# Attention scores on four array quarters and two PSUM banks, with a new order of products, new ordering rules and a table of due times

## The chip, the cores and the metric

One core of a Trainium2 chip runs the whole program. The metric is device time in microseconds (us): 1652.56, the median of three runs (1651.66 to 1653.05).

## The reference

```python
# q, k, v: 8 batches x 8 heads x 576 tokens x 64, float32
scores = scale * (q_chunk @ k_chunk.T)        # chunks of 64 tokens, 9 per head
attn = exp(scores - max); attn = attn / (sum(attn) + 1e-9)
x = (attn @ v_chunk), as 4608 tokens x 512
h = maximum(x @ moe_w_in, 0)                  # 512 x 2048
y = (h * h) @ moe_w_out                       # 2048 x 512
gate = 1 / (1 + exp(-(y @ moe2_w_gate)))      # 512 x 1536
out = (gate * (y @ moe2_w_val)) @ moe2_w_out  # 1536 x 512, result 4608 x 512
```

## The kernel before

Everything is first written down as jobs (`Plan.job`): an engine, an estimated cost, the buffers read and written, and for TensorE (PE) work a nominal time. `Plan.run` plays these jobs through on its own estimates, once, while the kernel is built, and so fixes one order per engine and the SBUF and PSUM places of all buffers; `Plan.emit` then issues them in that order. PE work comes in two streams: "main", the big products, taken in the order written, and "att", the attention jobs, each with a nominal time counted in main-stream work. At every free moment of PE the ready candidate with the smallest due time goes. The other engines take the ready job with the smallest due time; a job that must place a new buffer waits until it is near its due time (`LOOK`, `NEAR`). All DMAs are issued from SP's queue (L415), in that one order.

**Attention** (`attention`): 36 tiles of 128 tokens, two chunks of 64 each. For q and k of the first tiles, four PE transposes (L768) turn the data; later tiles are loaded in a shape that VectorE (DVE) turns (L751; such a load, `ql` or `kl`, is 16 DMAs). Then come the scores (L785, 16 products of 64x64x64, each two matmul records, so 32 records a tile, into one PSUM bank), on DVE the maximum (L803) and the subtraction (L804), Exp on ScalarE (ACT, L806), sum and normalisation on DVE (L807 to L812), a transpose on PE (L819), a copy (L422), the product with v (L835, "mix", also 32 records, but on all four quarters of the array and in two banks), and two copies into `raw` (L850). `raw` holds the tokens of a pair of blocks: 6 tiles, 768 tokens. The scores use, for either chunk c and head half r, the array rows of half r and the output partitions of half r: two diagonal quarters.

**The main stream.** The first pair of blocks runs as plain products (`plain_unit`) against the weights `wia` and `wil`, while the weights are still being turned from 64-bit words into float32 and split in two fp32r parts. The other pairs run as Strassen-like units of seven products P1 to P7 (`Unit`, L641; six matmuls of 384 columns each in the first stage, 512 or 256 columns in the gate and value stage). Bank U of a unit collects P1, P6, P7 and P4 one on the other; after P6 ACT copies it to `c`, after P7 DVE adds it to `b` (L451), so P7 must wait for the copy and P4 for the addition. `units` interleaves a unit with the last one: P1, P7 of the last, P2, P5, P3 and P4 of the last, P6. The two w_out stages (`Long`, L961) do the same seven products, each over all k parts, in the order P1, P4 of the last, P2, P5, P6, P3, P7; P7 and P4 need a difference of inputs from POOL (or DVE), P3 and P2 need none. Stages in time: start-up to 35 us, plain products to about 123, first units to 501, `Long` to 850, gate and value units to 1380, `Long` to the end.

## Time and profile before

| | |
|---|---|
| time, median of 3 runs | 1652.56 us |
| span of the profiled execution | 1649.1 us |
| PE busy | 1614.4 us, 98% |
| DVE busy | 1363.8 us, 83% |
| ACT, POOL busy | 983.6 us, 817.1 us |
| granted TensorE clock, mean | 0.994 |

The profile is of one execution, whose span runs from the first to the last instruction. Matmuls are pipelined and their ends are modelled, so what a piece of PE work costs is read from the distance between starts, not from the busy time. What ended a wait is inferred from semaphore events.

### The profile page before, as it was taken

How to read it: one execution, taken by the hardware profiler on the slowest of the kernel's cores; microseconds unless marked ns; L12 is line 12 of the kernel's file. 1: busy time of each engine (PE TensorE's matmuls, PEld its weight loads, DVE VectorE, ACT ScalarE, POOL GpSimd, SP SyncE). 2: the span in 40 equal slices, each digit the busy share in tenths (PEclk: the TensorE clock that was granted, in tenths of full speed). 3: DMA queues.
4: the chain of work that ended last, by engine and by line, in shares of the span. 5: the costliest groups of instructions: out<-in, count | busy, mean ns of one | idle time of the engine just before them, and what ended most of it. 6: DMA issues, size and time to landing. Idle time of an engine off the chain costs nothing.

```text
span 1649.1 us, 30839 instructions
## 1 busy us (share of the span) xinstructions
PE 1614.4 (98%) x10500; PEld 1459.8 (89%) x10500; DVE 1363.8 (83%) x2002; ACT 983.6 (60%) x1968; POOL 817.1 (50%) x636
## 2 busy tenths in 40 slices
PE   7999999999999999999999999999999999999998
PEld 6998998999999999999988888888888888788887
DVE  6988885777769999999999897754787737999995
ACT  6876765666666565566666565544564545455543
POOL 1253412030334444544469786643676637767672
PEclk9999999999999999999999999999999999999999
DMA  9955666577674765675865846496456687665562
GB/s 226 274 153 143 164 194 170 159 207 193 215 261 156 220 200 176 222 235 194 315 218 205 287 152 208 157 356 226 152 174 217 204 318 246 178 197 128 165 174 47
DMA packets 390798, 333.36 MB, mean 202 GB/s; under 512 B 234736, under 2 KB 325616, under 8 KB 390640
## 3 DMA queue, kind: packets, MB, share of 16 engines
q1 hardware_dynamic: 390640, 331.38, 65.1%
q8 instruction: 83, 1.36, 0.4%
q14 instruction: 75, 0.61, 0.1%
HBM read 209.13 MB, written 122.16 MB: 201 GB/s over the span
## 4 chain that ended last, share of the span: by engine, by line
PE 87%; DVE 6%; SPq 2%; issue 2%; DMA 1%; ACT 1%; POOL 1%; DVEq 0%; ACTq 0%
PE bank L641 47%; PE bank L961 35%; SPq L415 2%; PE bank L785 2%; PE bank L835 1%; PE bank L819 1%; PE bank L768 1%; DMA wraw__378<-in_moe_w_in_dram 0%; DVE T__2002 L442 0%; DMA gd<-b__2597 0%; DMA gd<-b__4693 0%; DMA g__6282<-gd 0%; DVE T__1999 L442 0%; DVE T__10402 L442 0%; DVE x__14497 L442 0%
## 5 line engine op out<-in xcount | busy, mean ns | idle before, releaser
L507 POOL TENSOR_TENSOR wf__1799<-wf__1799,wr__1407 128x512 int32<-128x512 int32 x16 | 21.2, 1325 | 181.6 <-DVE wf__1799 L500 85.1
L507 POOL TENSOR_TENSOR wf__7363<-wf__7363,wr__6457 128x512 int32<-128x512 int32 x18 | 26.1, 1450 | 79.1 <-ACT x__8870 L437 19.4
L507 POOL TENSOR_TENSOR wf__6801<-wf__6801,wr__6457 128x512 int32<-128x512 int32 x18 | 27.2, 1509 | 66.3 <-DVE wf__6801 L500 45.3
L451 POOL TENSOR_TENSOR raw__514<-raw__674,raw__514 128x384 f32<-128x384 f32 x20 | 23.6, 1202 | 42.4 <-DVE B__741 L442 26.7
L488 ACT ACTIVATE wr__6457<-wr__6457 128x512 int32<-128x512 uint32 x36 | 23.9, 664 | 0.0
L442 DVE TENSOR_TENSOR wx__7300<-ws__7420,wx__7300 128x512 fp32r<-128x512 f32 x18 | 19.0, 1053 | 0.0
L491 DVE TENSOR_SCALAR wf__7363<-wf__7363 128x512 f32<-128x512 f32 x18 | 10.4, 576 | 10.0 <-ACT wf__7363 L484 10.0
L442 DVE TENSOR_TENSOR wx__7585<-ws__7420,wx__7585 128x512 fp32r<-128x512 f32 x18 | 18.3, 1017 | 0.0
L451 POOL TENSOR_TENSOR ws__7420<-wf__6801,wf__7363 128x256 f32<-128x256 f32 x18 | 16.7, 928 | 2.3 <-DVE wx__7585 L442 1.1
L500 DVE SCALAR_TENSOR_TENSOR wf__7363<-wr__6457,wf__7363 128x512 int32<-128x512 int32 x18 | 16.2, 901 | 0.1
L491 DVE TENSOR_SCALAR wf__6801<-wf__6801 128x512 f32<-128x512 f32 x18 | 10.6, 588 | 6.8 <-ACT wf__6801 L484 6.8
L507 POOL TENSOR_TENSOR w__647<-w__647,wraw__374 128x512 int32<-128x512 int32 x1 | 1.3, 1294 | 29.9 <-DVE w__647 L500 29.9
L451 POOL TENSOR_TENSOR ws__7420<-ws__7420,wf__6801 128x256 f32<-128x256 f32 x18 | 15.4, 857 | 1.3
L442 DVE TENSOR_TENSOR wx__7423<-wf__7363,wx__7423 128x256 fp32r<-128x256 f32 x18 | 14.4, 801 | 1.8 <-ACT wx__7423 L437 1.8
L493 DVE TENSOR_SCALAR wf__7363<-wf__7363 128x512 int32<-128x512 int32 x18 | 14.5, 807 | 0.6
L484 ACT ACTIVATE wf__6801<-wr__6457 128x512 f32<-128x512 f32 x18 | 12.0, 666 | 5.0 <-POOL ws__7420 L451 2.3
L484 ACT ACTIVATE wf__1799<-wr__1407 128x512 f32<-128x512 f32 x16 | 10.6, 663 | 4.3 <-DMA wf<-wf__1799 4.2
L500 DVE SCALAR_TENSOR_TENSOR wf__6801<-wr__6457,wf__6801 128x512 int32<-128x512 int32 x18 | 12.8, 713 | 0.1
L850 ACT ACTIVATE raw__514<-bank 128x256 f32<-128x256 f32 x36 | 12.0, 384 | 1.0 <-PE bank L835 0.5
L484 ACT ACTIVATE wf__7363<-wr__6457 128x512 f32<-128x512 f32 x18 | 11.8, 656 | 1.1 <-DVE wx__7423 L442 0.9
L451 POOL TENSOR_TENSOR raw__514<-raw__514 128x384 f32<-128x384 f32 x10 | 12.4, 1260 | 0.0
L850 ACT ACTIVATE raw__674<-bank 128x256 f32<-128x256 f32 x36 | 11.9, 380 | 0.2
(5702 smaller groups left out, 6477.2 us busy)
## 6 DMA issues: line engine op xcount, KB each, us to landing
ad<-wx__7300 SPq DMA_DIRECT2D x27, 512.0 KB, 4.6
ad<-wx__7585 SPq DMA_DIRECT2D x27, 512.0 KB, 4.1
wr__1407<-in_moe_w_out_dram SPq DMA_DIRECT2D x16, 512.0 KB, 4.4
wr__6457<-in_moe_w_gate_dram SPq DMA_DIRECT2D x12, 512.0 KB, 5.4
wr__6457<-in_moe_w_val_dram SPq DMA_DIRECT2D x12, 512.0 KB, 5.6
wr__6457<-in_moe_w_out_dram SPq DMA_DIRECT2D x12, 512.0 KB, 4.1
ad<-wx__7423 SPq DMA_DIRECT2D x18, 256.0 KB, 4.4
wf<-wf__1799 SPq DMA_DIRECT2D x16, 256.0 KB, 4.6
```

What stands on the lines that cost most here:

```text
L415: nc.sync.dma_start(out=a, in_=b)
L442: lambda: nc.vector.tensor_tensor(out=lo(), in0=at(src, n, F32, off), in1=hi().bitcast(F32), op=ALU.subtract),
L451: eng, cost(eng, n), lambda: e.tensor_tensor(out=o(), in0=a(), in1=b(), op=op),
L484: nc.scalar.activation(out=at(w), in_=t[:, :, 1].bitcast(F32), func=ACTF.Abs)
L488: nc.scalar.activation(out=low, in_=low.bitcast(U32), func=ACTF.Copy, scale=2.0**-29)
L491: nc.vector.tensor_scalar_max(at(w), at(w), TINY)
L500: nc.vector.scalar_tensor_tensor(out=wi, in0=words()[:, :, 1], scalar=-0x40000000, in1=wi, op0=ALU.bitwise_and, op1=ALU.bitwise_or,)
L507: nc.gpsimd.tensor_tensor(out=wi, in0=wi, in1=words()[:, :, 0], op=ALU.add)
L641: nc.tensor.matmul(out=o, lhsT=at(op, P, F32R, wi * size + half * HB + kk * P), rhs=at(xb, n, F32R, xi * xsize + off), start=(first and kk ...
L785: nc.tensor.matmul(out=o[part, 2 * hp + c, :], lhsT=qv[part, hp, tok], rhs=kv[part, hp, tok], start=True, stop=True,)
L850: nc.scalar.activation(out=o[:, :, a:a + CH], in_=i, func=ACTF.Copy)
L961: nc.tensor.matmul(out=at(ps[m], n), lhsT=at(w, P, F32R, wi * size + half * HB + m * P), rhs=at(x, n, F32R, xi * n), start=(first and kp = ...
```

## The change

It has seven parts. (1) The scores of chunk c go to a bank of their own, and the second chunk's products cross over: array rows of half r, output partitions of half 1 - r; the four products of one head pair stand next to each other. Maximum and subtraction become two operations each, on 256 columns; the mix reads its weights from the crossed places. (2) The planner adds a cost when PE goes from full-array to quarter products and back (`ENTER`, `LEAVE`), and while in quarter products prefers another such job that is up to 6 us early (`STAY`). (3) A load or store on SP that is not due within 10 us is held while the estimated DMA backlog is over 2 us (`CALM`, `DEEP`). (4) The nominal times of the attention jobs come from a table, and a mix waits as a job for the readers of `raw` and for the mix before. (5) `units` takes P2 ahead of P7 of the last unit, and the last unit and the end of a stage have an order of their own; so has the last unit of `long_units`. (6) The plain products read their second weight from the place of `t`, whose real contents, with `s` and `d`, are made after the plain unit; the buffer `wil` goes. (7) The token operands of the first stage are placed ahead of everything.

```diff
@@ -135,7 +135,7 @@
         events, order = [], []
         t, dma, shift, done = 0.0, 0.0, 0.0, 0
         port = {"DVE": 0.0, "POOL": 0.0, "debt": 0.0}
-        stall, why = 0.0, {}
+        small = False
 
         def place(b):
 
@@ -194,7 +194,7 @@
             return False
 
         def begin(j):
-            nonlocal dma, done, shift
+            nonlocal dma, done, shift, small
             j.start, j.started = t, True
             done += 1
             order.append(j)
@@ -206,7 +206,10 @@
 
 
                 cost = j.cost
-                if j.shared and j.eng == "DVE":
+                if j.eng == "PE":
+                    cost += self.ENTER * (j.shared and not small) + self.LEAVE * (small and not j.shared)
+                    small = j.shared
+                elif j.shared and j.eng == "DVE":
                     cost += port["debt"] + min(0.82 * cost, 0.45 * max(0.0, port["POOL"] - t))
                     port["debt"], port["DVE"] = 0.0, t + cost
                 elif j.shared:
@@ -231,7 +234,7 @@
                         cands = [jobs[n] for _, n in ready["PE"]]
                         if heads["main"] < len(streams["main"]):
                             cands.append(jobs[streams["main"][heads["main"]]])
-                        for j in sorted(cands, key=lambda j: j.due):
+                        for j in sorted(cands, key=lambda j: (j.due - self.STAY * (small and j.shared), j.n)):
                             if not j.left and take(j):
                                 if j.stream == "main":
                                     heads["main"] += 1
@@ -253,8 +256,8 @@
                         j = jobs[n]
                         tries += 1
                         need = sum(b.size for b in j.allocs if b.at is None)
-                        ok = True
-                        if need:
+                        ok = not (e == "SP" and due - t + shift > self.CALM and dma - t > self.DEEP)
+                        if need and ok:
                             if due - t + shift > (j.look or (self.LOOK if e == "SP" else self.NEAR)):
                                 ok = False
                             else:
@@ -305,7 +308,9 @@
         self.order = order
         return order
 
-    LOOK, NEAR, HOLD, FAR, FLOOR = 90.0, 20.0, 8.0, 55.0, 8 * 1024
+    LOOK, NEAR, HOLD, FAR, FLOOR = 90, 20, 8, 55, 8192
+    ENTER, LEAVE, STAY = 0.1, 0.15, 6
+    CALM, DEEP = 10.0, 2.0
 
     def stuck(self, t, free, ready, heads, streams, shift):
         live = {}
@@ -574,25 +579,28 @@
             return lambda: at(buf, HB, F32, i * HB)
 
         finished("a")
+
+        def rest(look):
+            s1, s2, s3, s4 = ((sums, i) for i in range(4))
+            for o, x, y, op in (
+                (s1, a21, a22, ALU.add),
+                (s2, s1, a11, ALU.subtract),
+                (s3, a11, a21, ALU.subtract),
+                (s4, a12, s2, ALU.subtract),
+            ):
+                binary("POOL", part(*o), part(*x), part(*y), op, HB, [sums],
+                       {x[0], y[0]} | ({sums} if o[1] else set()), look=look)
+            split(ops["s"], sums, BLK, look=look)
+            finished("s")
+            split(ops["t"], sums, BLK, off=BLK, look=look)
+            finished("t")
+            split(ops["d"], b, HB, off=HB, look=look)
+            finished("d")
+
         if late:
-            ops["l"] = Buf(8 * BLK, name="wil", op=True)
-            split(ops["l"], b, BLK, look=look)
-            look = late
-        s1, s2, s3, s4 = ((sums, i) for i in range(4))
-        for o, x, y, op in (
-            (s1, a21, a22, ALU.add),
-            (s2, s1, a11, ALU.subtract),
-            (s3, a11, a21, ALU.subtract),
-            (s4, a12, s2, ALU.subtract),
-        ):
-            binary("POOL", part(*o), part(*x), part(*y), op, HB, [sums],
-                   {x[0], y[0]} | ({sums} if o[1] else set()), look=look)
-        split(ops["s"], sums, BLK, look=look)
-        finished("s")
-        split(ops["t"], sums, BLK, off=BLK, look=look)
-        finished("t")
-        split(ops["d"], b, HB, off=HB, look=look)
-        finished("d")
+            split(ops["t"], b, BLK, look=look)
+            return ops, lambda: rest(late)
+        rest(look)
         return ops
 
     def weight_rows(src, f, name, keep=True, look=None, raws=None):
@@ -753,6 +761,46 @@
             job("DVE", 0.1 + 0.15 * n, go, [r], [o])
             i += n
 
+    TIMES = [
+        (-40, -40, -38, -34, -32),
+        (-38, -38, -36, -32, -30),
+        (-36, -36, -34, -30, -28),
+        (-34, -34, -32, -28, -26),
+        (-32, -32, -30, -26, -24),
+        (-30, -30, -28, -24, -22),
+        (19.5, 15, 17.5, 21.5, 23),
+        (-0.75, 9, 0.25, 3.25, 26.5),
+        (20.25, 15.25, 20.5, 13, 27.5),
+        (24.25, 25.25, 30.5, 27, 30),
+        (13.75, 19.75, 13.5, 24.5, 28.5),
+        (19.75, 30.5, 36.25, 38.25, 52),
+        (69.25, None, 51.5, 67.5, 72.25),
+        (70.25, None, 64.75, 65.5, 72.5),
+        (82.5, None, 83.5, 88.75, 92.75),
+        (88.485, None, 89.526, 94.731, 98.895),
+        (96.75, None, 94.75, 100.25, 105.75),
+        (96.5, None, 96.5, 102.75, 105),
+        (126.25, None, 131.75, 132.25, 134.5),
+        (136, None, 139.75, 149.75, 150),
+        (131.75, None, 142, 145.75, 144.5),
+        (149, None, 156.75, 160.5, 161.75),
+        (155.25, None, 156, 157.25, 169),
+        (160.75, None, 157, 166.75, 172.5),
+        (186.5, None, 188.75, 187.75, 192.5),
+        (191, None, 200, 203.5, 208.5),
+        (184.75, None, 189, 200.75, 206.25),
+        (203.5, None, 204.5, 209.75, 216.25),
+        (217.75, None, 211.75, 212.25, 225.75),
+        (224.75, None, 222.5, 232, 229),
+        (253.25, None, 250.25, 254.75, 264.25),
+        (242.5, None, 240.25, 255.25, 259),
+        (251.25, None, 255.75, 264.75, 276),
+        (272.75, None, 265.25, 278, 288.75),
+        (255, None, 261, 278.25, 285.25),
+        (276.25, None, 275.5, 291, 289),
+    ]
+    before_mix = []
+
     def attention(t, raw, col, nominal):
         turned = {}
         for src, nm in ((k, "k"), (q, "q")):
@@ -769,28 +817,31 @@
                         out=at(ps, P, F32, hp * P), in_=at(r, P, F32, hp * P), identity=ident
                     )
 
-            job("PE", 0.45, go, [r], [ps], stream="att", at=nominal("k"))
+            job("PE", 0.45, go, [r], [ps], stream="att", at=nominal(nm))
             copy(lambda o=o: at(o), [o], lambda ps=ps: at(ps, BLK), [ps], BLK)
         qT, kT = turned["q"], turned["k"]
-        ps = psum("ps_s")
+        ps_s = [psum(f"ps_s{c}") for c in range(2)]
+
+        def chunk(c):
+            return at(ps_s[c], HB).rearrange("p (h k) -> p h k", h=HP)
 
         def scores():
             qv, kv = (at(x).rearrange("p (h t) -> p h t", h=HP) for x in (qT, kT))
-            o = at(ps, BLK).rearrange("p (h c) -> p h c", h=H)
-            for c in range(2):
-                tok = slice(CH * c, CH * c + CH)
-                for hp in range(HP):
+            o = [chunk(c) for c in range(2)]
+            for hp in range(HP):
+                for c in range(2):
+                    tok = slice(CH * c, CH * c + CH)
                     for r in range(2):
-                        part = slice(CH * r, CH * r + CH)
+                        part, to = (slice(CH * x, CH * x + CH) for x in (r, r ^ c))
                         nc.tensor.matmul(
-                            out=o[part, 2 * hp + c, :],
+                            out=o[c][to, hp, :],
                             lhsT=qv[part, hp, tok],
                             rhs=kv[part, hp, tok],
                             start=True,
                             stop=True,
                         )
 
-        job("PE", 1.0, scores, [qT, kT], [ps], stream="att", at=nominal("S"))
+        job("PE", 0.53, scores, [qT, kT], ps_s, stream="att", at=nominal("S"), shared=True)
         mx = sbuf(128, "mx")
         a = sbuf(BLK, "a")
 
@@ -800,9 +851,19 @@
         def col8(b, i):
             return at(b, H, F32, i * H).rearrange("p (h o) -> p h o", o=1)
 
-        job("DVE", 0.7, lambda: nc.vector.tensor_reduce(out=col8(mx, 0), in_=heads(ps), axis=AX.X, op=ALU.max), [ps], [mx])
-        job("DVE", 0.7, lambda: nc.vector.tensor_tensor(
-            out=heads(a), in0=heads(ps), in1=col8(mx, 0).to_broadcast([P, H, CH]), op=ALU.subtract), [ps, mx], [a])
+
+        def largest(c):
+            return at(mx, HP, F32, c * HP).rearrange("p (h o) -> p h o", o=1)
+
+        def of_chunk(c):
+            return at(a, BLK).rearrange("p (h c k) -> p h c k", h=HP, c=2)[:, :, c, :]
+
+        for c in range(2):
+            job("DVE", 0.45, lambda c=c: nc.vector.tensor_reduce(
+                out=largest(c), in_=chunk(c), axis=AX.X, op=ALU.max), [ps_s[c]], [mx])
+            job("DVE", 0.35, lambda c=c: nc.vector.tensor_tensor(
+                out=of_chunk(c), in0=chunk(c), in1=largest(c).to_broadcast([P, HP, CH]), op=ALU.subtract),
+                [ps_s[c], mx], [a])
         job("ACT", 0.63, lambda: nc.scalar.activation(out=at(a), in_=at(a), func=ACTF.Exp, scale=scale), [a], [a])
         job("DVE", 0.7, lambda: nc.vector.tensor_reduce(out=col8(mx, 1), in_=heads(a), axis=AX.X, op=ALU.add), [a], [mx])
 
@@ -835,12 +896,15 @@
                         nc.tensor.matmul(
                             out=o[c][CH * r:CH * r + CH, hp, :],
                             lhsT=vv[part, 2 * hp + r, :],
-                            rhs=av[part, hp, r, :],
+                            rhs=av[part, hp, r ^ c, :],
                             start=True,
                             stop=True,
                         )
 
-        job("PE", 0.8, mix, [aT, vr], ps_x, stream="att", at=nominal("X"))
+        mixed = job("PE", 0.66, mix, [aT, vr], ps_x, stream="att", at=nominal("X"), shared=True)
+        mixed.deps.update(raw.readers)
+        mixed.deps.update(before_mix)
+        before_mix[:] = [mixed.n]
         off = (t % TILES) * P
 
         def put(c):
@@ -903,7 +967,7 @@
         for row, col in ((0, 0), (1, 0), (0, 1), (1, 1)):
             ps = psum("C")
             for half in range(2):
-                multiply(ps, ops["al"[row]], half, xs[f"B{half + 1}{col + 1}"], n, half == 0, per)
+                multiply(ps, ops["at"[row]], half, xs[f"B{half + 1}{col + 1}"], n, half == 0, per)
             finish(u, row, col, ps)
 
 
@@ -911,7 +975,13 @@
         last = None
         for make in [*todo, None]:
             u, more = make() if make is not None else (None, None)
-            for who, p in ((u, "P1"), (last, "P7"), (u, "P2"), (u, "P5"), (last, "P3"), (last, "P4"), (u, "P6")):
+            if u is None:
+                steps = [(last, p) for p in ("P2", "P7", "P3", "P4")]
+            elif make is todo[-1]:
+                steps = [(u, "P1"), (u, "P5"), (last, "P7"), (last, "P3"), (u, "P6"), (last, "P4")]
+            else:
+                steps = [(u, "P1"), (u, "P2"), (last, "P7"), (u, "P5"), (last, "P3"), (last, "P4"), (u, "P6")]
+            for who, p in steps:
                 if who is not None:
                     who.stage(p)
                 if p == "P4" and more is not None:
@@ -1014,7 +1084,10 @@
         last = None
         for make in [*todo, None]:
             u = make() if make is not None else None
-            for who, p in ((u, "P1"), (last, "P4"), (u, "P2"), (u, "P5"), (u, "P6"), (u, "P3"), (u, "P7")):
+            steps = [(u, "P1"), (last, "P4"), (u, "P2"), (u, "P5"), (u, "P6"), (u, "P3"), (u, "P7")]
+            if make is todo[-1]:
+                steps = [(u, "P1"), (last, "P4"), *((u, p) for p in ("P5", "P6", "P2", "P7", "P3"))]
+            for who, p in steps:
                 if who is not None:
                     who.stage(p)
             last = u
@@ -1066,18 +1139,11 @@
         SLOT = 6 * per1
         raw1 = [sbuf(KD * BL1, f"raw{c}", top=True) for c in range(2)]
         slots1 = {name: [Buf(8 * BL1, top=True, name=name, op=True) for _ in range(2)] for name in B_OF.values()}
-        WHEN = {"k": 0, "S": 1, "T": 6, "X": 10}
-
+        plan.first.extend(b for some in (slots1.values() if isinstance(slots1, dict) else slots1) for b in some)
         def attend(s):
-            for i in range(2 * TILES):
-                def nominal(what, i=i):
-                    slot = 7 * i + WHEN[what]
-                    if s == 0:
-                        return -40.0 + 2.0 * i + {"k": 0, "S": 2, "T": 6, "X": 8}[what]
-                    if s == 1:
-                        return slot * SLOT * 8 / 7
-                    return span0 + (s - 2) * span + slot * SLOT
-                attention(2 * TILES * s + i, raw1[i // TILES], i // TILES, nominal)
+            for t in range(2 * TILES * s, 2 * TILES * (s + 1)):
+                i = t % (2 * TILES)
+                attention(t, raw1[i // TILES], i // TILES, dict(zip("kqSTX", TIMES[t])).get)
 
         def blocks1(raws):
             return {(r, c): [(raws[c], (2 * r + kk) * BL1) for kk in range(2)] for r in range(2) for c in range(2)}
@@ -1104,10 +1170,11 @@
             for op, (src, off) in zip(first_xs[name], x):
                 split(op, src, BL1, off=off)
         for g in range(G1):
-            w1[g] = weight_group(w1i, g, G1, f"wi{g}", True, look=30.0, late=30.0)
+            w1[g], rest = weight_group(w1i, g, G1, f"wi{g}", True, look=30.0, late=30.0)
             if g == 1:
                 attend(1)
             plain_unit(w1[g], first_xs, BL1, per1, finish0(g))
+            rest()
         state = {}
 
         def unit1(s, g):
```

## Rows read from the trace of the kernel before

**Rows 1.** Page: busy us, share, instructions.
```profile
PE 1614.4 (98%) x10500; PEld 1459.8 (89%) x10500; DVE 1363.8 (83%) x2002; ACT 983.6 (60%) x1968; POOL 817.1 (50%) x636
```

**Rows 2.** Windows: stretch, length, busy us by engine, clock, DMA share, GB/s.
```profile
34.70:131.00 96.30, 94.97 (x930) 89.05 (x928) 88.43 (x146) 77.65 (x160) 42.52 (x38) 1.00 0.78 208
131.00:440.00 309.00, 302.17 (x2976) 284.44 (x2977) 233.14 (x442) 199.09 (x434) 68.47 (x62) 0.99 0.66 183
...
70.00:80.00 10.00, 10.00 (x115) 9.37 (x114) 9.84 (x15) 8.36 (x18) 4.38 (x4) 1.00 1.06 317
```

**Rows 3.** Timeline of PE around scores: start, length, what, records.
```profile
208.37 0.69 PE L641 MATMUL bank<-T__2050,wid__2730 128*128 128x384 f32 x3
208.99 1.15 PE L785 MATMUL bank<-kT__1941,qT__2812 64*64 64x64 f32 x32
210.06 0.79 PE L641 MATMUL bank<-T__1999,wis__1503 128*128 128x384 f32 x3
210.70 0.68 PE L641 MATMUL bank<-T__2002,wis__1503 128*128 128x384 f32 x3
211.22 0.68 PE L641 MATMUL bank<-B__741,wia__861 128*128 128x384 f32 x3
```

**Rows 4.** Timeline of PE around a mix.
```profile
218.53 0.69 PE L641 MATMUL bank<-T__2002,wis__1597 128*128 128x384 f32 x3
219.14 0.69 PE L835 MATMUL bank<-aT__643,v__2931 64*64 64x64 f32 x32
219.76 0.79 PE L641 MATMUL bank<-B__741,wia__1015 128*128 128x384 f32 x3
220.40 0.68 PE L641 MATMUL bank<-B__744,wia__1015 128*128 128x384 f32 x3
```

**Rows 5.** Windows of the scores' line L785: PE, PEld, clock, DMA, GB/s.
```profile
34.70:440.00 405.30, 35.27 (x960) 31.10 (x960) 0.99 0.69 189
```

**Rows 6.** Waits of PE: us in total, times, longest.
```profile
PE bank L785 <- ACT kT__2177 L422: 3.9, 1, 3.9
PE bank L961 <- ACT x__8116 L437: 3.5, 1, 3.5
...
PE bank L641 <- DVE T__2002 L442: 1.6, 3, 0.8
PE bank L641 <- DVE b__11090 L451: 1.4, 1, 1.4
...
PE bank L641 <- ACT c__2138 L422: 0.8, 1, 0.8
...
PE bank L641 <- ACT c__10973 L422: 0.2, 1, 0.2
```

**Rows 7.** Timeline of all engines, 277 to 290 us.
```profile
277.90 5.43 SPq L415 DMA_DIRECT2D ql__3745<-in_q_dram  x11
...
287.50 0.49 ACT L422 ACTIVATE b__2597<-bank 128x384 f32<-128x384 f32 x1 [6.90 <-DMA gd<-b__2597]
...
289.35 1.98 PE L785 MATMUL bank<-kT__2177,qT__3890 64*64 64x64 f32 x32 [3.86 <-ACT kT__2177 L422]
```

**Rows 8.** Timeline, 845 to 847 us: DVE and PE.
```profile
845.59 0.54 DVE L451 TENSOR_TENSOR b__8437<-b__8437,bank 128x384 f32<-128x384 f32 x1
846.23 1.28 PE L961 MATMUL bank<-x__6308,wod__6323 128*128 128x384 f32 x6 [3.50 <-ACT x__8116 L437]
```

**Rows 9.** Timeline, 979 to 985 us: PE and DVE, units of 256 columns.
```profile
979.91 0.98 PE L641 MATMUL bank<-T__10970,v__9698 128*128 128x256 f32 x6
...
983.97 0.41 DVE L451 TENSOR_TENSOR b__11090<-b__11090,bank 128x256 f32<-128x256 f32 x1
...
984.43 0.38 PE L641 MATMUL bank<-T__10993,v__9685 128*128 128x256 f32 x1 [1.38 <-DVE b__11090 L451]
```

**Rows 10.** Windows of the maximum's line L803: DVE busy us.
```profile
0.00:1649.00 1649.00, 24.81 (x36) 0.99 0.66 202
```

**Rows 11.** Chain of work that ended last, 0 to 40 us: start, length, what.
```profile
24.45 6.11 DMA wraw__378<-in_moe_w_in_dram
```

## Prediction

> **What bounds the kernel now.** I read the busy table first: PE is busy 98% of the span, DVE 83%, ACT 60%, POOL 50% [rows 1]. An engine at 98% with the full clock (1.00 in the stretches of rows 2) leaves two ways to a shorter time: less PE work, or fewer PE waits. The table of PE waits comes next [rows 6]: after start-up no cause is above 4 us, and the idle times of PE from 36 to 1637 us, added up, are some 17 us. So the question for each part is how many microseconds of PE's own queue it takes away, and whether what feeds PE can follow. The windows answer the second: DVE is busy 88.4 of 96.3 us in the stretch of the plain products and 233 of 309 us in the units behind it [rows 2]. The first 35 us are no PE stage: their chain runs through SP's queue into the loads of q, k, v and the first weights, the last a load of 6.1 us [rows 11].
>
> **What the scores cost PE.** Undisturbed main groups of three matmuls start 0.52 us apart (210.70, 211.22) [rows 3]. From the start of the last main group ahead of the scores (208.37) to the second group behind them (210.70) are 2.33 us, of which two groups are 1.04; the scores cost 1.29 us. By the same count the mix costs 220.40 - 218.53 - 1.04 = 0.83 us [rows 4], with the same 32 records of 64 columns. Inside, the scores' records start (1.15 - 0.22)/31 = 0.030 us apart, taking 0.22 us as the modelled end of the last, the mix's (0.69 - 0.22)/31 = 0.015: two at a time against four. So 0.96 us of the scores is 32 records at their pace and 0.33 us entering and leaving; of the mix 0.48 and 0.35. The new order gives the scores the mix's pattern, four quarters and two banks. They should cost 0.83 us, 0.46 less. 960 records, 30 tiles, lie among main work [rows 5]: **30 x 0.46 = 13.8 us less**. The other six lie in start-up, where the loads set the end; I count them at nothing (between -2 and +2 us).
>
> Here a rule of the Trainium skill speaks against the change. "TensorEngine Tiling (Array Packing)", PSUM Pressure, says that different row tiles can't access the same PSUM bank simultaneously; the new order sends both row halves into each bank. By it the pairs of a bank would go one after the other and nothing of the 13.8 us would come. The old scores do just that already, both row halves into one bank, and their records start as densely as two at a time [rows 3]; the trace doesn't bear the rule out, for outputs on different partitions.
>
> **Scores and mixes side by side.** The visits stand alone today, each paying its 0.33 to 0.35 us of entering and leaving [rows 3, 4]. With `STAY` a second quarter job that is ready and up to 6 us early follows at once. From the table's due times of tiles 6 to 35, 60 jobs, I counted groups: 33 if all are ready, 45 if data take 3 us more to be ready. So 15 to 27 visits fall away. No row shows two of them side by side; the saving for each lies between nothing and 0.35 us. I take 18 at 0.30, nearer the upper end, because the cost sits at the change between the two kinds and not inside: **-5.4 us** (0 to -9.5). The same page, Key Properties, says that changing the tiling mode drains the engine; by it the whole 0.35 is saved and the sum is 0.9 us lower.
>
> **The order of the products.** P7 waits for ACT's copy of U after P6 (the `c` waits). Between P6 and P7 stands one product, P1; with P2 moved ahead there are two. Six `c` waits, 0.8 down to 0.2 us, sum 3.1 (the first and the last stand in [rows 6]); one more product (1.04 us or more; 0.79 in narrow units, below) covers each, also at the end of the stages, where P4 and P2 come between. **-3.1 us**. The price: P4 waits for DVE's addition after P7 (the `b` waits), and its cover falls from three products to two. There are four such waits, sum 2.5, the longest 1.4 us [rows 6]. In that one P7 starts at 979.91, DVE gets to the addition at 983.97, and P4 starts at 984.43 after 1.38 us of idling [rows 9]; a product there takes (4.52 - 1.38)/4 = 0.79 us. If DVE comes no earlier, each of the three in narrow units grows by 0.79, and a few in wide ones begin: up to +4. The planner's due time for the addition moves ahead with P4, so I take **+1.9** (0 to +4).
>
> **The last `Long` unit.** P4 follows P7 directly, so it waits for both additions: DVE begins the first at 845.59, and P4 starts at 846.23 after 3.50 us idle [rows 8]. The new order puts P3 between, which needs no difference from POOL and lasts over 8 us. **-3.5 us**, and what is next there, P4's differences from POOL, gains the time of P3 too. At the kernel's end the same swap changes who is second last, not the last chain: nothing.
>
> **SP's queue.** The longest PE wait, 3.9 us, begins in SP: 16 small loads of `ql`, 11 of them in 5.4 us, stand ahead of the stores; ACT waits 6.9 us for a store to free its buffer, PE for ACT, and the scores behind it take 1.98 us [rows 7] instead of 1.15 [rows 3]: 4.7 us in all. Holding what isn't urgent should take this one away, but every order is new and the estimates that missed here will miss elsewhere: I count half, **-2.4** (0 to -5).
>
> **What DVE takes back.** Maximum and subtraction are 36 operations of 0.69 us each [rows 10]; four of 256 columns at 0.41 [rows 9] are 1.64 in place of 1.38 us, 0.26 more a tile, 9 us at most over the kernel. Behind 131 us the 25% of free DVE time hides it. In the stretch to 131 us there are 7.9 us free [rows 2], the slice 70 to 80 has 0.2, with DMA at 1.06 of its share there, and the units behind it already wait for DVE at the start of a pair (one operand, three waits, 1.6 us) [rows 6]. PE's saving there is 6 x 0.46 and some 1.5 for neighbours, 4.3 us; with 1.6 more DVE work little of the 7.9 is left. I give back half: **+2.3** (0 to +5). The other parts are free: reading `wil`'s contents from `t` moves the same two splits, and making `s`, `t`, `d` after the plain unit takes work from the full stretch into one with room.
>
> **The sum.** -13.8 - 5.4 - 3.1 + 1.9 - 3.5 - 2.4 + 2.3 = -24.0. From the span of 1649.1 to 1625.1; the runs lie 3.5 above the span of the profiled execution, so 1652.6 - 24.0 = **1628.6 us**.
>
> **Rivals.** First, only the quarters count: the neighbours save nothing, the `b` waits grow to +4, a stall like that in SP's queue comes back. -13.8 - 3.1 + 4 - 3.5 + 2.3 = -14.1, 1638.5. For it: no row shows the price of a neighbour, and the planner's estimates missed at 289 us. Against: each piece is a bound, and they would have to fall together. Chance 0.19. Second, all of it: 27 neighbours at 0.35, no SP stall, DVE's additions earlier, nothing taken back: -13.8 - 9.5 - 3.1 - 3.5 - 5 = -34.9, 1617.7. Against it stands DVE's full stretch. 0.12. Third, the bank rule holds and the scores stay at 1.29 us: -24.0 + 13.8 = -10.2, 1642.4; against it, the old scores' pace. 0.05. Fourth, **slower**: the hold starves the plain products. In that stretch DMA is at or over its share for long, a weight load takes 6.1 us to land at the start [rows 11], and eight weight groups follow each other. If SP holds a load while the estimated backlog is over 2 us, and lets it go 10 us ahead, landing, four operations and the splits don't fit in any more; PE then waits for each group. From 24.0/8 = 3.0 us a group on, all is eaten; at 4 us it is 1660. Against: a held load waits only behind loads that keep the engines busy, and urgent ones pass. 0.04. A time within 0.2% has 0.02, the forecast's own 1622 to 1636 has 0.58.
>
> **How the numbers follow.** About 0.2%, 3.3 us, is what a measurement of this kernel can tell from no change. Faster: 0.58 + 0.19 + 0.12 + 0.05 = 0.94; same 0.02; slower 0.04. The range reaches from the second rival with a little room, 1616, past the first and the third to 1645.
>
> **What would show it.** The scores at 0.69 us a visit like the mix, and 15 or more visits with two or more jobs: right; scores at 1.15: the bank rule. The `c` waits and the wait at 846 us gone, `b` waits perhaps longer. The waits for T operands at the first unit show what DVE takes back, waits for weights ahead of 120 us the starving. The forecast is wrong if PE's waits add up to over 30 us, whatever their place.

## The result and the profile after

The changed kernel takes 1635.03 us (median of four runs, 1634.46 to 1635.46), the kernel before 1652.8 in the same runs: a ratio of 0.9897, interval 0.9884 to 0.9911. The span of the profiled execution fell from 1649.1 to 1633.7 us, by 15.4; the other 2.4 us of the medians' 17.8 lie between single executions and stand in no trace.

The first lines of the page after, to be read beside [rows 1]:

```profile
span 1633.7 us, 30814 instructions
...
PE 1599.7 (98%) x10500; PEld 1445.2 (88%) x10500; DVE 1376.7 (84%) x2074; ACT 974.6 (60%) x1968; POOL 817.1 (50%) x636
```

PE does as many matmuls as before and is busy 14.7 us less; DVE has 72 instructions and 13 us more. PE is as full as it was, so its work and its waits must be told apart. A visit is a piece of PE's queue in which only quarter products (scores and mixes) stand. The timeline of PE around one visit of the scores (L836), and around two scores side by side, each between main groups (L649):

```profile
106.57 0.69 PE L649 MATMUL bank<-B__760,wia__1690 128*128 128x384 f32 x3
107.18 0.69 PE L836 MATMUL bank<-kT__1731,qT__1609 64*64 64x64 f32 x32
107.81 0.79 PE L649 MATMUL bank<-B__640,wit__1672 128*128 128x384 f32 x3
108.44 0.68 PE L649 MATMUL bank<-B__648,wit__1672 128*128 128x384 f32 x3
...
239.76 0.69 PE L649 MATMUL bank<-T__2081,wid__2453 128*128 128x384 f32 x3
240.38 0.69 PE L836 MATMUL bank<-kT__2483,qT__3372 64*64 64x64 f32 x32
240.89 0.65 PE L836 MATMUL bank<-kT__3091,qT__3325 64*64 64x64 f32 x32
241.47 0.79 PE L649 MATMUL bank<-T__2024,wis__2315 128*128 128x384 f32 x3
242.10 0.68 PE L649 MATMUL bank<-T__2026,wis__2315 128*128 128x384 f32 x3
```

The scores have the mix's 0.69 us of [rows 4] in place of 1.15 [rows 3]. One visit costs 108.44 - 106.57 less the 1.04 us of two main groups (three matmuls of 0.1735 us each), so 0.83 us. Two side by side cost 242.10 - 239.76 less the same, so 1.30 us: a neighbour saves the whole entering and leaving, 0.36 us.

With these prices the stretch from the first main matmul to the last matmul of the first units can be taken apart in any of the kernels: 2063 matmuls of 0.1735 us (357.8), quarter work (0.93 or 0.47 us of records for scores, 0.47 for a mix, 0.36 for each visit), full-array transposes of 0.434 us (27.8 or 28.2), and a **rest**, which is mostly waits of PE and time lost at the lower clock. The kernel before has 60 visits, 63.6 us of quarter work and a rest of 17.3; the changed kernel 47 visits, 44.9 us and a rest of 23.4. Quarter work gave 18.7 us, the rest took 6.1 back. In this stretch PE idles 10.1 us before and 13.3 after (of it 3.9 and 11.0 until DVE is done, 6.0 and 1.2 until ACT is), and the granted clock is at its lower level (0.50, that is 1.2 in place of 2.4 GHz) for some 8 us before and some 16 after; so the clock has about as large a part in the 6.1 as the waits. Each rest here and below is read from one execution, and the executions of one kernel lay between 1.0 us (the changed kernel) and 10.3 us apart, so a difference of a few us in a rest shows little by itself. By stage, before and after, in us:

| stage | before | after |
|---|---|---|
| to the first main matmul | 34.7 | 33.4 |
| plain products | 88.1 | 90.3 |
| first units | 378.5 | 364.3 |
| first `Long` | 353.3 | 353.4 |
| gate and value units | 524.6 | 520.4 |
| second `Long` to the end | 269.8 | 272.0 |

The waits of PE after, to be read beside [rows 6] (L649 is the units' matmul, L880 the transpose of the attention weights, L1031 `Long`, L816 the transposes of q and k; us in total, times, longest):

```profile
PE bank L649 <- DVE b__3715 L456: 2.5, 1, 2.5
PE bank L649 <- DVE T__2024 L447: 2.1, 2, 1.9
PE bank L880 <- DVE a__1976 L873: 2.0, 1, 2.0
PE bank L649 <- DVE wia__751 L447: 1.6, 1, 1.6
PE bank L649 <- DVE b__4287 L456: 1.1, 1, 1.1
...
PE bank L1031 <- DVE x__6506 L447: 0.8, 1, 0.8
```

No `c` copy is left among PE's waits, and the 3.5 us ahead of P4 in `Long` are gone. In their place DVE is late. At three of these waits the clock falls, to 0.50 for 3.4 us each (from 131.2, 271.2 and 431.6 us); the windows of 4 us around them (length, busy us of PE, PEld, DVE, ACT and POOL, clock, DMA share, GB/s):

```profile
129.00:133.00 4.00, 2.41 (x10) 1.61 (x10) 3.96 (x5) 2.20 (x6) 4.00 (x4) 0.78 0.22 49
269.00:273.00 4.00, 3.20 (x14) 3.20 (x15) 3.96 (x10) 2.52 (x6) 0.04 (x1) 0.77 0.62 227
429.50:433.50 4.00, 2.06 (x7) 1.66 (x8) 4.00 (x6) 3.05 (x8) 3.62 (x3) 0.76 0.91 290
```

DVE is busy for all of each window, at 129 and 429 beside a busy POOL. What it does at 125 to 131 us, in the timeline (some rows of DVE and POOL, and the PE group that waits):

```profile
125.42 0.55 DVE L447 TENSOR_TENSOR T__799<-raw__510,T__799 128x384 fp32r<-128x384 f32 x1
...
125.58 2.24 POOL L456 TENSOR_TENSOR raw__510<-raw__679,raw__510 128x384 f32<-128x384 f32 x2 [4.35 <-DVE T__789 L447]
...
126.22 0.55 DVE L456 TENSOR_TENSOR e__1791<-bank,e__1791 128x384 f32<-128x384 f32 x1
...
127.77 1.96 POOL L456 TENSOR_TENSOR raw__679<-raw__679 128x384 f32<-128x384 f32 x2
127.86 0.94 DVE L871 TENSOR_SCALAR mx__1973<-mx__1973 128x8 f32<-128x8 f32 x1
...
129.08 1.20 DVE L873 TENSOR_TENSOR a__1976<-a__1976,mx__1973 128x512 f32<-128x512 f32 x1
129.68 2.75 POOL L456 TENSOR_TENSOR raw__510<-raw__510 128x384 f32<-128x384 f32 x2
130.21 1.36 DVE L447 TENSOR_TENSOR T__2024<-raw__510,T__2024 128x384 fp32r<-128x384 f32 x1
130.43 0.63 PE L880 MATMUL bank<-ident,a__1976 128*128 128x128 f32 x4 [2.05 <-DVE a__1976 L873]
```

The split of 384 columns that starts ahead of POOL's subtractions takes 0.55 us, the one that starts in the middle of one 1.36, and an operation on eight columns 0.94 (0.16 or 0.17 in 32 of the 36 tiles). Not all of DVE is slowed: the addition at 126.22, which reads a PSUM bank, takes its usual 0.55 us beside POOL. The ends suggest that the slow operations wait for POOL's running instruction: the one on eight columns ends at 128.81 us, the subtraction beside it at 128.78. No run tried this by itself. The wait at 270 us begins elsewhere, in SP's queue:

```profile
253.46 9.46 SPq L420 DMA_DIRECT2D ql__3653<-in_q_dram  x16
263.02 0.40 SPq L420 DMA_DIRECT2D gd<-e__2302  x1
...
264.92 0.71 DVE L759 STREAM_TRANSPOSE qT__3773<-ql__3653 128x512 f32<-128x512 f32 x1 [2.29 <-DMA gd<-e__2302]
...
269.21 0.54 DVE L456 TENSOR_TENSOR b__3715<-b__3715,bank 128x384 f32<-128x384 f32 x1
269.80 0.79 PE L649 MATMUL bank<-T__2072,wid__2665 128*128 128x384 f32 x3 [2.49 <-DVE b__3715 L456]
```

The 16 DMAs of this `ql` load are planned at 7.2 us and take 9.46. DVE turns the load at 264.92, after 2.29 us idle; the view puts this down to a store that SP issued right behind the load, and the load's last piece landed at 264.5. DVE then does four splits, two of them beside POOL, and only then the addition that P4 waits for.

### The profile page after: what moved, and what is told of

Its sections match the earlier page's. It is cut to its first block, busy times and chain, and to the rows that moved or that the text cites. A ratio compares the mean times of both kernels' runs of the same rounds, so it can differ in the third digit from the quotient of the medians.

```text
span 1633.7 us, 30814 instructions
## 1 busy us (share of the span) xinstructions
PE 1599.7 (98%) x10500; PEld 1445.2 (88%) x10500; DVE 1376.7 (84%) x2074; ACT 974.6 (60%) x1968; POOL 817.1 (50%) x636
## 3 DMA queue, kind: packets, MB, share of 16 engines
q8 instruction: 83, 1.36, 0.4%
## 4 chain that ended last, share of the span: by engine, by line
PE 84%; DVE 9%; DMA 2%; issue 2%; ACT 1%; POOL 1%; SPq 1%; DVEq 0%; POOLq 0%; ACTq 0%
PE bank L649 46%; PE bank L1031 35%; PE bank L836 1%; PE bank L816 1%; PE bank L896 1%; DMA wraw__1337<-in_moe_w_in_dram 1%; PE bank L880 1%; SPq L420 1%; DMA gd<-c__4078 0%; DMA v__9966<-ad 0%; DMA k__299<-in_k_dram 0%; POOL ws__7533 L456 0%; DMA k__4752<-in_k_dram 0%; POOL wf__7203 L512 0%; DMA ud<-s__10228 0%
## 5 line engine op out<-in xcount | busy, mean ns | idle before, releaser
L498 DVE TENSOR_SCALAR wf__7203<-wf__7203 128x512 int32<-128x512 int32 x18 | 17.4, 968 | 0.6
L456 POOL TENSOR_TENSOR ws__7533<-ws__7533,wf__7000 128x256 f32<-128x256 f32 x18 | 15.8, 877 | 1.2
L447 DVE TENSOR_TENSOR wx__7485<-wf__7203,wx__7485 128x256 fp32r<-128x256 f32 x18 | 13.3, 737 | 3.1 <-ACT wx__7485 L442 3.1
L498 DVE TENSOR_SCALAR wf__7000<-wf__7000 128x512 int32<-128x512 int32 x18 | 14.2, 791 | 0.6
L914 ACT ACTIVATE raw__679<-bank 128x256 f32<-128x256 f32 x36 | 11.8, 384 | 2.4 <-PE bank L896 2.2
```

The source lines that it names most:

```text
L447: lambda: nc.vector.tensor_tensor(out=lo(), in0=at(src, n, F32, off), in1=hi().bitcast(F32), op=ALU.subtract),
L456: eng, cost(eng, n), lambda: e.tensor_tensor(out=o(), in0=a(), in1=b(), op=op),
L498: nc.vector.tensor_scalar(out=wi, in0=wi, scalar1=5, scalar2=2, op0=ALU.logical_shift_left, op1=ALU.logical_shift_right,)
```

## The experiments

Theories: (Q) PE's own queue sets the time, and the quarters and neighbours come off it; (D) VectorE takes the gain back, by its additional work or by running late beside POOL; (S) SP's queue behind the `ql` and `kl` loads is late; (P) the plan as a whole decides: parts put into another order meet other waits. Ratios are to the kernel before on the same chip; the changed kernel has 0.9897.

**The quarters alone.** In the kernel before, with nothing else of the change but the scores' order and planned cost, the new second operations on DVE and the mix reading the crossed places:

```diff
                     for r in range(2):
-                        part = slice(CH * r, CH * r + CH)
+                        part, to = (slice(CH * x, CH * x + CH) for x in (r, r ^ c))
...
-                            out=o[part, 2 * hp + c, :],
+                            out=o[c][to, hp, :],
```

> The kernel before with one part alone: scores on four quarters and two banks, two maxima and two subtractions, the mix reading the crossed weights. Theory (PE's queue sets the time): 30 tiles x 0.45 us come off, 1652.8 - 13.6 = 1639, within 4 us of it for the waits of a new plan. Rival (DVE takes it back, with 0.26 us more a tile): above 1645, with the waits of PE for DVE 6 us or more longer.

Measured 1670.0 us, ratio 1.0113 (1.0095 to 1.0130): slower. Quarter work fell as computed, from 63.6 to 47.8 us (55 visits). In the profiled execution the rest rose from 17.3 to 43.4, and the first `Long`, which has no attention in it, took 14 us more (367.4). This execution, at 1677.3 us, was the slowest of five and 7.3 above their median, so a part of these increases is its own. PE's longest waits from 34 to 520 us:

```profile
PE bank L832 <- DVE a__1302 L825: 3.6, 1, 3.6
PE bank L641 <- ACT e__2885 L422: 2.6, 1, 2.6
PE bank L641 <- DVE T__1987 L442: 2.6, 3, 1.8
PE bank L641 <- ACT c__2866 L422: 2.5, 2, 1.9
PE bank L788 <- ACT kT__2121 L422: 2.3, 1, 2.3
```

Q falls for this plan. Of D the signs came: the time is above 1645, and up to the last matmul of the first units PE waits 12.7 us for DVE in place of 3.9. Its cause, 0.26 us more of DVE a tile, doesn't cover what is seen: ACT is waited for 13.8 us in place of 6.0, and `Long` is longer without any tile. The jobs' costs and banks changed, and with them the whole plan; in this execution the rest of that plan cost 1.7 times what the quarters gave. It speaks for P.

**The same plan with the old quarters.** The changed kernel, both banks kept, only the cross-over undone:

```diff
-                        part, to = (slice(CH * x, CH * x + CH) for x in (r, r ^ c))
+                        part, to = (slice(CH * x, CH * x + CH) for x in (r, r))
...
-                            rhs=av[part, hp, r ^ c, :],
+                            rhs=av[part, hp, r, :],
```

> The changed kernel with the same plan, instruction for instruction, but the scores' products on the two diagonal quarters again (still two banks). Theory: the scores cost 1.29 us in place of 0.83 wherever they stand, so 30 x 0.45 = 13.6 us are lost, 1648.6. Rival (PE waits for DVE anyway in this stage): the longer scores fill waits, which shrink from 23 us to under 18, and only 8 us or less are lost, 1643.

Measured 1643.7 us, ratio 0.9959 (0.9944 to 0.9974): 0.0062, some 10 us, slower than the changed kernel. Quarter work is 58.9 us, 14.0 more, and the rest 15.8, 7.6 less. In the timeline the scores at 246 us:

```profile
246.00 1.15 PE L836 MATMUL bank<-kT__2483,qT__3372 64*64 64x64 f32 x32
```

So the quarters are worth 14.0 us of PE's time under one and the same plan, and some 4 us of that by the medians, 7.6 by the traces, are lost again in the rest. PE idles 10.0 us in the stretch in place of 13.3, and of the three falls of the clock at 131, 271 and 431 us only the first is left; behind the wait at 439 us, as long as the one at 431 (1.92 against 1.95), it stayed at 1.00. The median lies between the two expectations, on the side of the second, and the rest came down as the second had it.

**No preference for a neighbour** (`STAY` from 6 to 0).

> The changed kernel without the preference for a second quarter job (0 us in place of 6). Theory (each neighbour saves 0.36 us of entering and leaving): 13 neighbours go, 4.7 us are lost, 1639.7. Rival (the new plan's waits decide, neighbours are worth little): anywhere from 1632 to 1640 with no relation to the number of visits.

Measured 1653.3 us, ratio 1.0016 (1.0006 to 1.0026). Six visits more (53) are 2.2 us of quarter work; the rest is 32.8, 9.4 more, and the plain products take 103.1 in place of 90.3 us, among it one wait of 4.1 us for a load of k. Both expectations missed: seven neighbours stay without the preference, and the loss comes from the new plan's waits, beyond what the rival allowed. The price of a neighbour isn't tested by this run, since the plan isn't the same; it stands on the rows at 240 us.

**The old order of the units** (P1, P7 of the last, P2, P5, P3 and P4 of the last, P6).

> The changed kernel with the old order of the products in the units (P1, P7 of the last, P2, ...). Theory (a product of cover moved from P4 to P7): the c waits of some 3 us come back, most of them in the gate and value stage, whose 4.2 us of gain go; the b waits of 3.7 us in the first units go. Sum near nothing, 1635 +- 3. Rival (only the waits for DVE's addition matter): faster, 1631.

Measured 1646.0 us, ratio 0.9967 (0.9956 to 0.9977). The `c` waits are back, and longer than in [rows 6]; the `b` waits of the first units are gone:

```profile
PE bank L649 <- ACT c__5155 L427: 3.5, 1, 3.5
PE bank L649 <- ACT c__2722 L427: 2.4, 2, 1.7
...
PE bank L649 <- ACT c__10121 L427: 1.6, 1, 1.6
...
PE bank L649 <- DVE b__14185 L456: 0.4, 1, 0.4
```

The gate and value stage takes 524.5 us against 520.4: the 4.2 us that it had gained are gone, as expected. In the first units the exchange isn't even. ACT's lateness lands on P7, and the rest rises to 31.5. Both expectations missed: with this table of due times the new order pays by more than the terms of the sum. A table made for the old order wasn't tried.

**POOL's subtractions halved.** The changed kernel, same plan, the subtraction of token operands in the first units on half of the columns:

```diff
-                binary("POOL", part(oo), part(xx), part(yy), ALU.subtract, n, ...)
+                m = n // 2 if slots else n
+                ... nc.gpsimd.tensor_tensor(out=some(oo)(), in0=some(xx)(), in1=some(yy)(), op=ALU.subtract) ...
```

> The changed kernel, same plan, but POOL's subtractions of token operands in the first units work on half of their columns (so T operands are wrong in the other half). Theory (VectorE beside a busy POOL runs late): the waits at 130 us (2.05) and 431 us (1.95 and 0.41) and the low clock behind them go, 5 us faster than the changed kernel, ratio to before 0.9866. Rival (VectorE's own order sets these waits): within 1 us of the changed kernel, 0.9897.

Measured 1630.7 us, ratio 0.9875 (0.9860 to 0.9890). The rest falls from 23.4 to 18.3 us, by 5.1, and the operation on eight columns and the split run faster:

```profile
127.50 0.27 DVE L878 TENSOR_SCALAR mx__1973<-mx__1973 128x8 f32<-128x8 f32 x1
...
128.04 0.80 DVE L880 TENSOR_TENSOR a__1976<-a__1976,mx__1973 128x512 f32<-128x512 f32 x1
128.77 0.94 DVE L447 TENSOR_TENSOR T__2024<-raw__510,T__2024 128x384 fp32r<-128x384 f32 x1
```

The waits at 130 and 431 us are gone as such (0.97 is left at the first). Another grew: the `b` wait of 1.1 us at 318 is 3.55 us here (at 315), with the clock falling behind it. The trace shows D in this form: not DVE's work, but its pace beside POOL. The ratio's interval still touches that of the changed kernel, so the gain in time isn't shown, only that the two waits go.

**One DMA for 16.** The changed kernel, same plan, `ql` and `kl` loads as one DMA of the same size:

```diff
-        dma(lambda: both()[0], lambda: both()[1], writes=[r], ...)
+            return [at(r)], [src[b, 4 * (g % 2):4 * (g % 2) + 4].rearrange("h (x s) d -> (h x) (s d)", x=32)]
+        dma(lambda: one()[0], lambda: one()[1], writes=[r], ...)
```

> The changed kernel, same plan, but each ql or kl load is one DMA of the same bytes in place of 16 (from other places of q and k, so the scores are wrong). Theory (SP falls behind its plan while it issues the 16, about 7.9 us in place of the 7.2 planned, and VectorE then reaches the addition that P4 waits for too late): the waits at 270 us (2.49) and 318 us (1.06) and the low clock behind the first go, 5 us faster than the changed kernel, ratio 0.9866. Rival (P4's cover of two products is too short whatever SP does): 0.9897, b waits as before.

Measured 1628.2 us, ratio 0.9864 (0.9848 to 0.9880). The rest falls to 16.3, by 7.1. The `b` waits are three, the longest 0.5 us:

```profile
PE bank L649 <- DVE b__10295 L456: 0.5, 1, 0.5
...
PE bank L649 <- DVE b__3610 L456: 0.3, 1, 0.3
...
PE bank L649 <- DVE b__11214 L456: 0.2, 1, 0.2
```

So the cover of two products suffices when DVE isn't held by a late load; the two long `b` waits of the changed kernel come from these loads. S holds, as far as it goes: this kernel's loads also have larger pieces, and the run doesn't part issue time from landing time.

**The old order of the last `Long` unit** (P2, P5, P6, P3, P7, then P4).

> The changed kernel with the old order of the last unit in both w_out stages (P3, P7, P4). The plan is the same up to about 770 us. Theory (P4 right behind P7 waits for VectorE and POOL): the wait at the end of the first w_out stage comes back, 3.5 us slower, ratio 0.9918. Rival (POOL's backlog sets that end either way): 0.9897.

Measured 1639.8 us (1634.3 to 1642.3), ratio 0.9928 (0.9907 to 0.9948), 0.0031 slower. In the profile the first `Long` takes 355.4 against 353.4 us and the second 0.8 us more; another 1.3 us stands ahead of 488 us, where the plan is the same. So the profile gives the swap some 3 us, near the expected 3.5, but the mechanism isn't the expected one alone: the wait that is back at the stage's end is 1.47 us (at 836 us, for ACT's part of an operand), not 3.5. The two ratios' intervals overlap, and the four runs lie 8 us apart, so the size isn't shown.

**No hold on SP** (`CALM` so large that it never holds).

> The changed kernel without the hold on SP. Theory (the hold keeps SP free for the stores): VectorE and ACT wait longer for stores, PE's waits grow by 3 to 6 us, ratio 0.992. Rival (the hold starves the start and the plain products): the plain stage, 90.3 us in the changed kernel against 88.1 before, gets 2 us or more shorter, ratio 0.988.

Measured 1666.1 us, ratio 1.0092 (1.0077 to 1.0107): 31 us slower than the changed kernel. The rest is 47.2, and the plain products take 102.7 us. The longest wait, in the timeline of PE:

```profile
107.19 1.12 PE L816 MATMUL bank<-ident,k__787 128*128 128x128 f32 x4 [8.21 <-DMA k__787<-in_k_dram]
```

A load of k that PE needs comes 8.2 us late. The theory had the direction, but not the size (3 to 6 us) nor the place: the longest wait is for a load, not for something behind a store. The rival, which is the fear of my fourth rival in the prediction, is refuted for this plan's table: the hold doesn't starve the plain products, without it they starve.

**The loads from POOL's queue, and from ACT's.** The changed kernel, same plan:

```diff
-                nc.sync.dma_start(out=a, in_=b)
+                (by or nc.sync).dma_start(out=a, in_=b)        # by=nc.gpsimd, or nc.scalar, for ql and kl
```

> The changed kernel, same plan, the right result, but the 16 DMAs of each ql or kl load are issued from POOL's queue, not SP's. Theory (SP's lateness behind those loads is what costs the b waits at 270 and 318 us): as with one DMA, some 7 us faster than the changed kernel, ratio 0.986. Rival (POOL pays for it: its subtractions and VectorE beside it run late by the issue time): 0.99 or more, with longer waits for T operands.

> The same, but issued from ACT's queue, which is busy 60 percent and copies what PE waits for. Theory (the issue time, some 0.5 us a DMA, moves to ACT): ACT is held 8 us at each load, PE's waits for ACT grow, ratio 0.992 or more. Rival (issuing costs ACT little): as with one DMA, 0.986.

Measured 1690.7 us, ratio 1.0245 (1.0224 to 1.0266), from POOL; 1731.1, ratio 1.0492 (1.0474 to 1.0509), from ACT. The rest is 78.0 and 120.7. The issuing, in the timelines of the two:

```profile
119.25 9.76 POOL L420 DMA_DIRECT2D ql__1767<-in_q_dram  x16
```

```profile
162.99 8.21 ACTq L420 DMA_DIRECT2D ql__1767<-in_q_dram  x15
...
171.25 0.42 ACT L442 ACTIVATE wid__2202<-w__802 128x256 fp32r<-128x256 f32 x1 [8.20 <-DMA ql__1767<-in_q_dram]
```

The issue costs some 0.5 to 0.6 us a DMA wherever it stands, and holds the engine behind it: POOL's next operation starts at 129.03, right behind the 16, and ACT's at 171.25. The theory's gain didn't come from either queue.

**One small DVE operation less** (`tensor_scalar_add(..., 1e-9)` left out).

> The changed kernel, same plan, without the addition of 1e-9 to the sums (they are at least 1, so nothing changes in float32): one small VectorE operation less a tile, 0.17 us alone, 0.94 us beside POOL at 128 us. Theory (VectorE beside POOL sets the wait at 130 us): that wait falls from 2.05 to some 1.1 us, 1 to 3 us faster than the changed kernel, ratio 0.9885. Rival: within 0.5 us, 0.9897.

Measured 1632.2 us, ratio 0.9892 (0.9876 to 0.9907), not to be told from the changed kernel's. The rest of its profiled execution is 19.0 us, 4.4 less, which the ratio doesn't bear out: so far can one execution's rest lead astray. The wait itself did what was expected, 2.05 to 1.09 us:

```profile
128.91 0.63 PE L879 MATMUL bank<-ident,a__1963 128*128 128x128 f32 x4 [1.09 <-DVE a__1963 L872]
```

**The issue time planned as measured.** For `n == 16`, 0.59 us a DMA in the planner's estimate in place of 0.45.

> The changed kernel, right result, with one number of the planner's estimates changed: the 16 DMAs of a ql or kl load are planned at 0.59 us each (9.46 us for 16 in the changed kernel's trace) in place of 0.45. Theory (this estimate is what makes the b waits): the loads start earlier, the b waits at 270 and 318 us go, ratio 0.986 as with one DMA. Rival (every new plan has waits of its own, and the table of due times is made for this one): quarter work the same within 2 us, but PE's waits and slow stretches in the first 490 us, 23 us in the changed kernel, come to 28 us or more, ratio 0.992 or more.

Measured 1640.9 us, ratio 0.9943 (0.9922 to 0.9964): slower than the changed kernel. The `b` wait of 2.5 us is gone, and one of 1.0 is the longest left; the rest is 22.7, a little less. But an operand of the first units is now waited for 4.0 us (twice, 3.1 and 1.0), and the first `Long` takes 358.4 in place of 353.4 us. The mechanism is mended, the plan isn't better. The theory's ratio is refuted. The rival's came, not from the first 490 us where I had put it but from the stage behind.

## Why the prediction was right, and where it was off

The forecast was 1628.6 us, 24 less than before; measured are 17.8 less, inside the range and on the forecast's side. By its own steps:

- **The scores** (13.8): right. 30 tiles at the mix's price; under one plan, 14.0 us of PE's queue, of which some 10 reach the time. The bank rule of the Trainium skill ("TensorEngine Tiling (Array Packing)", PSUM Pressure) would have left the scores at 1.15 us; they take 0.69 with both row halves in each bank, on different partitions. The third rival is out.
- **Neighbours** (5.4, 18 at 0.30): 13 at 0.36, 4.7 us. Together with the scores 18.7 measured against 19.2. Twelve visits hold two or more jobs, not the 15 that I had named as a sign of being right. By the Trainium skill ("TensorEngine Tiling (Array Packing)", Key Properties) a change of the tiling mode drains the engine; the trace agrees in that the whole 0.36 us is saved.
- **`c` waits** (3.1): right, all gone.
- **`b` waits** (+1.9): they sum to 4.4 against 2.5 us, +1.9 as said, but that is luck: they are not where I said, in the narrow units, whose waits vanished, but most of them (2.5 and 1.1 us) in the first units. The run with one DMA in place of 16 takes the two long ones away.
- **The last `Long` unit** (3.5): the wait is gone, but the stage is as long as before (353.4 against 353.3 us): three waits for DVE's operands at its start (0.58, 0.65 and 0.83 us, with the slow matmuls beside them 3.2 in all) ate it. I had named P4's end and not asked what the new plan does to the beginning.
- **SP's queue** (2.4): the wait at 289 us went, 4.7 us, and came back as lateness at 270 and 318, in other clothes. Half was too generous: with one DMA the rest is 7.1 us lower. The 4.7 also left out the clock, which was at 0.50 from 288.2 to 295.0 us in the kernel before; the 1.98 us of the scores there were a part of that.
- **What DVE takes back** (+2.3): the mis-sized term. The additional operations cost what they should, 60.2 us against 49.7, 0.29 a tile against 0.26; but the full stretch wasn't their place. PE's waits for DVE grew from 3.9 to 11.0 us up to the end of the first units, most of them at three places with 2 to 2.5 us each, and in this execution the lower clock stood behind each of the three; with what other waits gave back, the rest rose by 6.1. I had priced DVE's free time and left out that some of its operations take more than twice their time beside POOL (1.36 for 0.55), and what the clock adds to a wait.
- **The second `Long`** (nothing): 2.2 us slower. Its products run at the pace of the pair POOL and DVE more often than before (17 of the 168 k parts at 1.6 to 1.8 us, in place of 7):

```profile
1447.43 1.74 POOL L456 TENSOR_TENSOR u__14436<-u__14170,u__14436 128x512 f32<-128x512 f32 x1
1447.94 1.77 DVE L447 TENSOR_TENSOR x__14712<-u__14821,x__14712 128x512 fp32r<-128x512 f32 x1
1449.10 1.86 PE L1031 MATMUL bank<-x__14712,o__14583 128*128 128x512 f32 x6
```

One k part each 1.7 us, where PE alone needs 1.36. Why the new plan falls into this more often wasn't tried.

My sign of being wrong, waits of PE of over 30 us in all, did not come: counted as in the prediction they are 14.8 us, against 16.8 before.

The sum's hidden assumption was that the other waits stay as they were. The runs show that they don't: with about the same quarter work (45 to 48 us), the rest went from 16 to 121 us over twelve kernels, and the quarters alone made the kernel slower. The forecast came out since the change brings due times, rules and orders that hold the rest at 23. Which of them is needed is shown only for the hold, the preference for a neighbour and the order, each taken out under a table made for all of them; the table itself, the place of `t` for the plain products and the early placing of the token operands weren't tried alone. And the steps aren't additive: of the 14.0 us of the quarters some 4 (by the medians) to 8 (by the traces) are lost again in the rest.

Of the runs that do the whole computation none is faster than the changed kernel. The one DMA, which loads other data, shows by its ratio some 5 us that are still to be had in the small loads; the halved subtractions hint at some 4 in the pace of DVE beside POOL, within the noise.

## What to carry to other kernels

Where one planner orders everything, price a change in two parts: the work that leaves the bounding engine, which can be counted to a few tenths, and the waits of the new plan, which no part of the old trace fixes; test a single edit under an unchanged plan before believing in its sum. Put four independent quarter products next to each other and keep the quarter jobs together: each visit cost 0.36 us for entering and leaving here. Look for operations of one engine that another slows, and for the clock behind a wait, before calling free time free.

## What the runs showed of the hardware that I had not expected

- A VectorE split beside POOL's subtractions took 1.36 in place of 0.55 us (384 columns) and 1.77 (512 columns), and even an operation on eight columns 0.94 in place of 0.17, or 0.27 with POOL's operations halved. An addition that read a PSUM bank kept its 0.55.
- A wait of PE of 2 to 2.5 us was followed by the lower clock (0.50 for 3.4 us, 0.76 to 0.78 over windows of 4 us) at three places of the changed kernel, but not every time: the wait of 1.92 us at 439 us with the old quarters and that of 2.25 at 271 us with the old last `Long` unit (the same plan up to there) had the clock at 1.00 behind them, and so had the 3.50 us at 846 us in the kernel before [rows 8].
- 16 DMAs of 36 KB took 7.9 to 9.5 us to issue from SP in the changed kernel, 9.6 to 11.4 from POOL and 8.0 to 12.8 from ACT, and from the last two the engine's own work waited behind them.
